# Grouped-query attention on one core: the order of the first loads, a query-major first group and zero matmuls at the start

## The chip, the core and the metric

The kernel runs on one core of a Trainium2 chip. The metric is the device time of one execution in microseconds (us), the median over several executions. Beside it stands one profiled execution, from which all durations of single instructions come. The engines are PE (matmul), ACT (activations), DVE (elementwise), POOL (elementwise) and SP (here it only issues DMAs).

## The reference

```python
B, Hq, Hkv, Sq, Sk, D = 16, 32, 8, 288, 512, 128      # q, k, v in bf16

def reference(q, k, v):
    rep = Hq // Hkv                                     # 4 query heads share one k/v head
    k = jnp.repeat(k, rep, axis=1)
    v = jnp.repeat(v, rep, axis=1)
    scores = jnp.einsum("bhqd,bhkd->bhqk", q, k) * D ** -0.5
    p = softmax(scores, axis=-1)
    return jnp.einsum("bhqk,bhkd->bhqd", p, v)
```

## The kernel before

**Groups and steps.** A group is one k/v head of one batch with its four query heads: 128 groups (`NG`), each with 4 x 288 = 1152 query rows (`R`, nine blocks of 128) against 512 keys (`NJ` = 4 blocks of 128). The transposed scores of a group have 4 x 1152 = 4608 columns (key block times query row). They are cut into three steps (`NC`) of 1536 columns (`CH`), so there are 384 steps (`NS`) in all. Four groups (`UG`) are a unit, which is what one load of keys and one of values brings (units are called `u`); the loads of unit 0 are split into single groups.

**One step.** For step `n` PE computes scores S(n) into one of two PSUM buffers (`op_s`, L499: four matmuls, or more where block borders cut them). ACT takes exp of all 1536 columns in one instruction into `pt_sb` (`op_exp`, L541). Then PE multiplies probabilities with values for three query blocks (`op_pv`, L522: 12 matmuls of 129 columns; the last column of `v_sb` is one and yields the softmax sum). DVE takes the reciprocal of the sums (`op_rc`, L558) and writes the scaled output (`op_ev`, L569). POOL copies values into `v_sb` beside the ones (`op_vc`, L551).

**Which columns a step has.** Steps go through the 4608 columns in key-major order: step 0 of a group has key block 0 with all 1152 queries and then a part of key block 1. The last group (`LASTG`) alone is query-major: each of its steps has 384 queries against all four key blocks (`pieces`, `op_exp`), which cuts its scores into six matmuls, so that its value steps can start after one exp each. Value steps of any other group wait for all three of its exps.

**The order on PE** is S(n), then the value step of `n - LAG`, with `LAG` = 4. S(n) waits for the group's keys and queries and for exp(n - 2), which frees its PSUM buffer.

**The order of the DMAs.** All DMAs are issued by SP in one order, and SP issues in order: an instruction that waits holds back those behind it. The list `first` (L601 to L603) has the loads of groups 0 to 3: `op_k(0, 0)`, `op_q(0)`, `op_k(0, 1)`, `op_q(1)`, `op_v(0, 0)` and so on. Then comes a branch into the main block. After it SP follows the list `sp`, which is sorted by a key written by hand in units of steps:

- keys `op_k(u)` (L432) and values `op_v(u)` (L444) of a unit, three buffers (`NSLOT`); from unit 3 on each waits for its buffer. Units 1 and 2 have keys near -24 + u, ahead of everything else.
- queries `op_q(g)` (L453, a transposing DMA of 128 x 1152), twelve buffers (`NQ`). Groups 4 to 11 have negative keys too.
- stores `op_store(g)` (L467), key `NC * (g + 1) + LAG + 1.5`: it waits for the group's evictions. The output has six buffers (`NO`), so the evictions of group 6 wait for store 0.

The sort key orders the issues; it is not a time at which they wait. There is a second path for extreme inputs (`general_path`), entered by a branch at the end and not taken in these runs.

Of the kernel before, what the change touches and what calls it, by code (L numbers as in the profile page):

```python
# [8 lines left out]
BF16 = mybir.dt.bfloat16  # L9
# [278 lines left out]
def bass_standalone__gqa_softmax__near_ridge_kernel(  # L288
# [6 lines left out]
    B, Hq, Sq, D = q.shape  # L295
    _, Hkv, Sk, _ = k.shape
    P = 128
# [7 lines left out]
    TPC = 3  # L305
# [9 lines left out]
    NSLOT = 3  # L315
    NQ = 12
    NPT = 3
    NO = 6
    NS = NG * NC
    LASTG = NG - 1  # L320
# [8 lines left out]
    with ExitStack() as es:  # L329
        sem = {}  # L330

        def S(name):
            if name not in sem:
                sem[name] = es.enter_context(nc.semaphore(name))
            return sem[name]
# [1 line left out]
        flag_i = es.enter_context(nc.sbuf_tensor("flag_i", [1, 1], I32))  # L337
        block = es.enter_context(nc.Block())

        for name in ["s_go", "s_one", "s_s", "s_e", "s_pv", "s_rc", "s_ev", "s_stat", "s_bad", "s_flag", "s_vc", "s_ol", "s_ea"]:  # L340
            S(name)
        for i in range(NSLOT):
            S("us_k%d" % i)
# [5 lines left out]
            S("s_q%d" % i)  # L349
        for i in range(NO):  # L350
            S("s_o%d" % i)


        gen = ExitStack()
# [4 lines left out]
        def general(eng, key, after):  # L359

            home[key] = nc.cur_bb
            eng.br(after + key)
            with nc.body("general_" + key):
                if key == "sp":
                    eng.sem_inc(sem["s_go"], 1)
                fns[key](eng)
                eng.br("done_" + key)
            nc.switch_bb(after + key)
# [27 lines left out]
        ck_sb = main.enter_context(nc.sbuf_tensor("ck_sb", [P, 3], FP32))  # L396
        bad_sb = main.enter_context(nc.sbuf_tensor("bad_sb", [P, 2, ALONE + 1], FP32))
        one_f = main.enter_context(nc.sbuf_tensor("one_f", [P, 1], FP32))
        dum = main.enter_context(nc.sbuf_tensor("dum", [P, 2], FP32))
        ps_s = main.enter_context(nc.psum_tensor("ps_s", [P, 2, CH], FP32))  # L400
        ps_o = main.enter_context(nc.psum_tensor("ps_o", [P, 2, BANK], FP32))
# [23 lines left out]
        def op_k(u, gi=None):  # L425
            eng = nc.sync
            sl = u % NSLOT
            if u >= NSLOT:
                for (s, n) in need(eng, [("s_s", NC * UG * (u - NSLOT + 1))]):
                    eng.wait_ge(s, n)  # L430
            g0, g1 = (0, UG) if gi is None else (gi, gi + 1)
            eng.dma_start_transpose(  # L432
                kt_sb[:, sl, :, g0:g1].rearrange("d j g p -> d j (g p)"),
                k_v[(u * UG + g0) * P:(u * UG + g1) * P]
            ).then_inc(sem["us_k%d" % sl if gi is None else "s_k%d" % gi], 16)
# [12 lines left out]
        def op_q(g):  # L448
            eng = nc.sync
            if g >= NQ:  # L450
                for (s, n) in need(eng, [("s_s", NC * (g - NQ + 1))]):
                    eng.wait_ge(s, n)
            eng.dma_start_transpose(qt_sb[:, g % NQ], q_v[g * P:(g + 1) * P]).then_inc(sem["s_q%d" % (g % NQ)], 16)  # L453

        def have(kind, g):

            u = g // UG
            if u == 0:
                return ("s_%s%d" % (kind, g), 16)
            return ("us_%s%d" % (kind, u % NSLOT), 16 * (u // NSLOT + (0 if u % NSLOT == 0 else 1)))  # L460
# [17 lines left out]

        def pieces(g, i):

            if g == LASTG:
                w = TPC * P
                cuts = sorted(set(range(0, CH + 1, BANK)) | set(range(0, CH + 1, w)))
                return [(a, a // w, i * w + a % w, b - a) for a, b in zip(cuts[:-1], cuts[1:])]
            lo, hi = i * CH, (i + 1) * CH
            cuts = sorted({lo, hi} | {x for x in range(0, COLS, BANK) if lo < x < hi}
                          | {x for x in range(0, COLS, R) if lo < x < hi})
            return [(a - lo, a // R, a % R, b - a) for a, b in zip(cuts[:-1], cuts[1:])]

        def op_s(n):  # L490
            eng = nc.tensor
            g, i = n // NC, n % NC
            sl, gi = (g // UG) % NSLOT, g % UG
            waits = [have("k", g), ("s_q%d" % (g % NQ), 16 * (g // NQ + 1))]
            if n >= 2:
                waits.append(("s_e", n - 1))
            qg = qt_sb[:, g % NQ].rearrange("d t p -> d (t p)")
            for x, (c, j, r0, w) in enumerate(pieces(g, i)):
                ins = emit(eng, waits if x == 0 else [], lambda: eng.matmul(  # L499
                    ps_s[:, n % 2, c:c + w], kt_sb[:, sl, j, gi, :], qg[:, r0:r0 + w], start=True, stop=True))  # L500
            ins.then_inc(sem["s_s"], 1)
# [27 lines left out]
        def op_exp(n):  # L529
            eng = nc.scalar  # L530
            g, i = n // NC, n % NC
            waits = [("s_s", n + 1)]
            if g >= NPT:
                waits.insert(0, ("s_pv", NC * (g - NPT + 1)))
            if g == LASTG:
                w = TPC * P
                dst = pt_sb[:, g % NPT].rearrange("p (j r) -> p j r", r=R)[:, :, i * w:(i + 1) * w]
                src = ps_s[:, n % 2].rearrange("p (j r) -> p j r", r=w)
            else:
                dst, src = pt_sb[:, g % NPT, i * CH:(i + 1) * CH], ps_s[:, n % 2]  # L540
            emit(eng, waits, lambda: eng.activation(dst, src, ACTF.Exp, scale=scale)).then_inc(sem["s_e"], 1)  # L541
# [56 lines left out]
                op0=ALU.is_lt, op1=ALU.add)).then_inc(sem["s_bad"], 1)  # L598


        first = [lambda: op_k(0, 0), lambda: op_q(0), lambda: op_k(0, 1), lambda: op_q(1), lambda: op_v(0, 0)]  # L601
        first += [lambda: op_k(0, 2), lambda: op_q(2), lambda: op_v(0, 1)]
        first += [lambda: op_k(0, 3), lambda: op_q(3), lambda: op_v(0, 2), lambda: op_v(0, 3)]  # L603

        sp = []
        for u in range(1, NU):
            t = NC * UG * (u - NSLOT + 1) if u >= NSLOT else -2 * NC * UG + u
            sp.append((t + 0.5, lambda u=u: op_k(u)))
            sp.append((t + (LAG if u >= NSLOT else 0.65), lambda u=u: op_v(u)))
        for g in range(UG, NG):  # L610
            t = NC * (g - NQ + 1) + 1.2 if g >= NQ else -2 * NC * UG + g // UG + 0.51 + 0.1 * (g % UG)
            sp.append((t, lambda g=g: op_q(g)))
        for g in range(LASTG):
            sp.append((NC * (g + 1) + LAG + 1.5, lambda g=g: op_store(g)))
# [4 lines left out]
        @block.sync  # L619
        def _(eng):  # L620
            for fn in first:
                fn()
            general(eng, "sp", "main_")
            for (_, fn) in sp:
                fn()
            choose(eng, "sp")

        @block.tensor
        def _(eng):
            for n in range(NS + LAG):  # L630
                if n == NS - 3:
                    hints["pe"] = eng.mark_branch_hint_location()
                if n < NS:
                    op_s(n)
                if n >= LAG:
                    op_pv(n - LAG)
            emit(eng, [("s_ev", NS - 1), ("s_bad", 2)], lambda: eng.matmul(  # L637
                ps_o[0:1, NS % 2, 0:ALONE + 1], one_f[:], bad_sb[:, 1, :], start=True, stop=True)
            ).then_inc(sem["s_bad"], 1)
            choose(eng, "pe", behind=True)  # L640

        @block.scalar
        def _(eng):
            emit(eng, [("s_one", 1)], lambda: eng.activation(dum[:, 1:2], dum[:, 0:1], ACTF.Exp))  # L644
            general(eng, "act", "main_")
            for n in range(NS):
                op_exp(n)
            op_ev_last()
            choose(eng, "act")
# [8 lines left out]

        @block.vector
        def _(eng):  # L660
            eng.memset(dum[:], 0.0).then_inc(sem["s_one"], 1)  # L661
            eng.memset(one_f[:], 1.0)
            general(eng, "dve", "main_")
            per_b = G * NC
            w0 = NS - 1 - ALONE // TPC
            last = rl_sb[:, NG * NT - ALONE:NG * NT]
            for r in range(NS):
                op_rc(r)
                op_ev(r)
                if r % per_b == per_b - 1 and r < NS - 1:  # L670
                    op_stat(r // per_b)
                if r == w0:
                    op_stat(B - 1)
                if r == w0 + 1:
                    emit(eng, [("s_stat", B)], lambda: eng.tensor_reduce(
                        ck_sb[:, 0:1], st_sb[:, 0, :], AX.X, ALU.max))
                    eng.tensor_reduce(ck_sb[:, 1:2], st_sb[:, 1, :], AX.X, ALU.min).then_inc(sem["s_stat"], 1)
                if r == w0 + 2:
                    op_over(ck_sb[:, 0:1], ck_sb[:, 1:2], ALONE, ALONE + 1, ("s_stat", B + 1), B + 2)
            op_over(last, last, 0, ALONE, ("s_rc", NS), B + 3)  # L680
            with nc.allow_low_precision(reason="a count of at most 2048"):
                emit(eng, [("s_bad", 3)], lambda: eng.tensor_reduce(  # L682
                    flag_i[:], ps_o[0:1, NS % 2, 0:ALONE + 1], AX.X, ALU.add)).then_inc(sem["s_flag"], 1)
            choose(eng, "dve")
# [30 lines left out]
```

## Time and profile before

| What | Value |
|---|---|
| median of 10 runs | 537.02 us (533.36 to 537.54) |
| the profiled execution | 537.76 us, of which its span from first to last instruction is 536.0 |
| PE busy | 521.5 us (97%), 6152 matmuls |
| ACT busy | 518.2 us (97%), 387 instructions |
| DVE busy | 288.3 us (54%) |
| POOL busy | 73.8 us (14%) |
| granted TensorE clock, mean | 0.994 |
| first score matmul | 6.86 us after the start of the span |
| HBM read and written | 16.78 MB and 37.75 MB |

In the page's second part the span is cut into 40 slices of 13.4 us, and each digit is the busy share of one slice in tenths; the row PEclk is the clock that TensorE was granted. Lines of the timeline begin with the start and the length in us; lines of waits give the total, the count and the longest. Where engines overlap, a long busy time says little by itself: what matters is which wait ended last.

### The profile page before, as it was taken

To read this page: it belongs to the slowest core of one execution; us is meant where nothing else is said; L and a number is where in the kernel's file an instruction comes from. 1 tells how busy PE (TensorE), PEld (TensorE's weight loads), DVE (VectorE), ACT (ScalarE), POOL (GpSimd) and SP (SyncE) were. 2 spreads that over 40 slices of the span, in tenths; PEclk is the share of its full clock that TensorE was granted. 3 is DMA by queue.
4 is the path that set the end of the run, shared out by engine and by line. 5 is a ranking of instruction groups with operands and counts; after the bars stand their busy time and mean duration, and the time that the engine had idled before them with its cause. 6 is when DMAs were issued, how large, how long until landed. Compare 5 with 4: busy or idle time off the path is not lost.

```text
span 536.0 us, 14538 instructions
## 1 busy us (share of the span) xinstructions
PE 521.5 (97%) x6152; PEld 406.2 (76%) x6152; DVE 288.3 (54%) x809; ACT 518.2 (97%) x387; POOL 73.8 (14%) x133
## 2 busy tenths in 40 slices
PE   4997999999999999999999999999999999999997
PEld 1775777777777777777777777777777777777776
DVE  0543555555555555555555555555555555555555
ACT  4995999999999999999999999999999999999996
POOL 1221111210111110111100111101111101111000
PEclk9997999999999999999999999999999999999999
DMA  7999999999899999999999999998989998985212
GB/s 135 209 194 255 243 237 257 289 244 221 200 204 225 224 223 202 182 222 222 231 214 174 228 209 223 225 202 223 197 212 224 232 194 227 187 217 159 89 68 91
DMA packets 253943, 110.07 MB, mean 205 GB/s; under 512 B 220848, under 2 KB 237616, under 8 KB 253872
## 3 DMA queue, kind: packets, MB, share of 16 engines
q1 hardware_dynamic: 253872, 109.08, 91.6%
q8 instruction: 50, 0.82, 0.7%
q14 instruction: 21, 0.17, 0.1%
HBM read 16.78 MB, written 37.75 MB: 102 GB/s over the span
## 4 chain that ended last, share of the span: by engine, by line
PE 96%; DMA 2%; DVE 1%; ACT 1%; SPq 0%; issue 0%; DVEq 0%
PE ps_o L522 49%; PE ps_s L499 47%; DMA qt_sb<-in_q_dram 1%; DMA out_dram<-o_sb 1%; ACT pt_sb L541 1%; DVE o_sb L569 0%; SPq L432 0%; SPq L453 0%; DVE rl_sb L558 0%; PE ps_o L637 0%; DVE bad_sb L596 0%; DVE flag_i L682 0%; DVE bad_sb L593 0%; DVEq L418 0%
## 5 line engine op out<-in xcount | busy, mean ns | idle before, releaser
L541 ACT ACTIVATE pt_sb<-ps_s 128x1536 bf16<-128x1536 f32 x384 | 516.4, 1722 | 12.0 <-PE ps_s L499 12.0
L522 PEld LDWEIGHTS ps_o<-v_sb,pt_sb 128*128 128x128 bf16 x4596 | 295.9, 98 | 59.0 <-DVE o_sb L569 4.2
L522 PE MATMUL ps_o<-v_sb,pt_sb 128*128 128x129 bf16 x4596 | 327.5, 221 | 3.8 <-DVE o_sb L569 3.8
L499 PE MATMUL ps_s<-qt_sb,kt_sb 128*128 128x512 bf16 (+3 forms) x1542 | 317.5, 329 | 7.6 <-DMA qt_sb<-in_q_dram 6.9
L569 DVE TENSOR_TENSOR o_sb<-ps_o,rl_sb 128x384 bf16<-128x384 f32 x383 | 213.6, 558 | 18.2 <-DMA out_dram<-o_sb 4.7
L558 DVE RECIPROCAL rl_sb<-ps_o 128x3 f32<-128x3 f32 x383 | 69.3, 181 | 226.3 <-PE ps_o L522 226.3
L499 PEld LDWEIGHTS ps_s<-qt_sb,kt_sb 128*128 128x128 bf16 x1542 | 117.6, 98 | 67.4 <-DMA qt_sb<-in_q_dram 6.9
L551 POOL COPY v_sb<-vd_sb 128x512 bf16<-128x512 bf16 x128 | 73.3, 616 | 417.5 <-DMA vd_sb<-in_v_dram 390.0
L588 DVE TENSOR_REDUCE st_sb<-rl_sb 128x1 f32<-128x72 f32 (+1 forms) x16 | 3.5, 217 | 0.0
L586 DVE TENSOR_REDUCE st_sb<-rl_sb 128x1 f32<-128x72 f32 (+1 forms) x16 | 3.5, 217 | 0.0
L577 ACT ACTIVATE o_sb<-ps_s,rl_sb 128x128 bf16<-128x128 f32 x1 | 0.4, 367 | 2.3 <-DVE rl_sb L558 2.3
L644 ACT ACT_TABLE_LOAD x1 | 1.3, 1283 | 0.8 <-PEq L700 0.8
L637 PE MATMUL ps_o<-bad_sb,one_f 128*1 128x25 f32 x2 | 0.2, 184 | 1.0 <-DVE bad_sb L596 1.0
L637 PEld LDWEIGHTS ps_o<-bad_sb,one_f 128*1 128x1 f32 x2 | 0.1, 80 | 1.2 <-DVE bad_sb L596 1.2
L522 PE MATMUL ps_s<-v_sb,pt_sb 128*128 128x129 bf16 x12 | 0.9, 221 | 0.0
L522 PEld LDWEIGHTS ps_s<-v_sb,pt_sb 128*128 128x128 bf16 x12 | 0.7, 98 | 0.0
L661 DVE MEMSET dum<- 128x2 f32 x1 | 0.1, 60 | 0.9 <-PEq L700 0.9
L569 DVE TENSOR_TENSOR o_sb<-ps_s,rl_sb 128x256 bf16<-128x256 f32 x1 | 0.4, 425 | 0.0
L653 POOL MEMSET v_sb<- 128x48 bf16 x1 | 0.3, 311 | 0.3 <-POOLq L700 0.3
L682 DVE TENSOR_REDUCE flag_i<-ps_o 1x1 int32<-1x25 f32 x1 | 0.2, 170 | 0.3 <-PE ps_o L637 0.3
L644 ACT ACTIVATE dum<-dum 128x1 f32<-128x1 f32 x1 | 0.2, 202 | 0.0
L596 DVE SCALAR_TENSOR_TENSOR bad_sb<-rl_sb,bad_sb 128x24 f32<-128x24 f32 x1 | 0.2, 184 | 0.0
(11 smaller groups left out, 1.4 us busy)
## 6 DMA issues: line engine op xcount, KB each, us to landing
out_dram<-o_sb SPq DMA_DIRECT2D x127, 288.0 KB, 3.4
vd_sb<-in_v_dram SPq DMA_DIRECT2D x31, 512.0 KB, 5.1
qt_sb<-in_q_dram SPq DMA_TRANSPOSE x128, 4.6
kt_sb<-in_k_dram SPq DMA_TRANSPOSE x35, 4.7
vd_sb<-in_v_dram SPq DMA_DIRECT2D x4, 128.0 KB, 3.1
out_dram<-o_sb SPq DMA_DIRECT2D x3, 96.0 KB, 1.6
```

The source lines that it names most:

```text
L499: ins = emit(eng, waits if x == 0 else [], lambda: eng.matmul(ps_s[:, n % 2, c:c + w], kt_sb[:, sl, j, gi, :], qg[:, r0:r0 + w], start=Tru ...
L522: ins = emit(eng, waits if a == 0 and j == 0 else [], lambda: eng.matmul(outs(r)[:, a, :], pt_sb[:, g % NPT, j * R + t * P:j * R + (t + 1) ...
L541: emit(eng, waits, lambda: eng.activation(dst, src, ACTF.Exp, scale=scale)).then_inc(sem["s_e"], 1)
L551: emit(eng, waits, lambda: eng.tensor_copy(v_sb[:, sl, gi * NJ:(gi + 1) * NJ, 0:D], vd_sb[:, sl, gi].rearrange("p (j d) -> p j d", d=D))). ...
L558: emit(eng, [("s_pv", r + 1)], lambda: eng.reciprocal(rl_sb[:, TPC * r:TPC * (r + 1)].unsqueeze(2), outs(r)[:, :, D:DV])).then_inc(sem["s_ ...
L569: emit(eng, waits, lambda: eng.tensor_tensor(out=o_sb[:, g % NO, t0:t0 + n, :], in0=outs(r)[:, 0:n, 0:D], in1=rl_sb[:, TPC * r:TPC * r + n ...
L577: emit(eng, [("s_o%d" % (LASTG % NO), 16 * (LASTG // NO)), ("s_rc", NS)], lambda: eng.activation(o_sb[:, LASTG % NO, NT - 1, :], outs(NS - ...
L586: emit(eng, [("s_rc", e // TPC)], lambda: eng.tensor_reduce(st_sb[:, 0, b:b + 1], rl_sb[:, a:e], AX.X, ALU.max))
L588: eng.tensor_reduce(st_sb[:, 1, b:b + 1], rl_sb[:, a:e], AX.X, ALU.min).then_inc(sem["s_stat"], 1)
L637: emit(eng, [("s_ev", NS - 1), ("s_bad", 2)], lambda: eng.matmul(ps_o[0:1, NS % 2, 0:ALONE + 1], one_f[:], bad_sb[:, 1, :], start=True, st ...
L644: emit(eng, [("s_one", 1)], lambda: eng.activation(dum[:, 1:2], dum[:, 0:1], ACTF.Exp))
L653: eng.memset(v_sb[:, :, :, D:DV], 1.0)
```

## The change

Five things are changed, all at the start of the execution:

1. **The sort keys of loads.** Each unit's keys and values and each group's queries get a key of at least about `NC * (g - 2.5) / 1.4`, so that the list brings loads 1.4 times as fast as steps use them, mixed with the stores. The new head of `sp` is: keys of unit 1 (3.01), values of unit 1 (3.16), queries of groups 4, 5, 6 (3.21, 5.36, 7.5), store 0 (8.5), queries 7 (9.64), store 1 (11.5), keys and values of unit 2 (11.59, 11.74), queries 8 and 9 (11.79, 13.93), store 2 (14.5). From group 31 on queries have the key of before; values of a unit from 3 on keep their distance of `LAG` to its keys.
2. **Group 0's queries** are loaded by three transposing DMAs of 384 columns with a semaphore each (`op_q0`, `have_q`), in place of one of 1152.
3. **Group 0 is query-major**, as the last group is: step i needs only piece i of the queries, and has six matmuls.
4. **Eight matmuls of zeros** (512 columns each) run on PE ahead of S(0), on a buffer that DVE clears first.
5. **ACT's branch** into the main block carries a branch hint, placed ahead of ACT's first activation.

```diff
+    WARM = 8
...
-            eng.br(after + key)
+            br = eng.br(after + key)
+            if key in hints:
+                br.branch_hint(hints[key])
...
+        z_sb = main.enter_context(nc.sbuf_tensor("z_sb", [P, BANK], BF16))
...
+        def op_q0(i):
+            c0, c1 = i * TPC, (i + 1) * TPC
+            nc.sync.dma_start_transpose(qt_sb[:, 0, c0:c1], q_v[0:P, c0 * D:c1 * D]).then_inc(sem["s_qp%d" % i], 16)
+
+        def have_q(g, i):
+            if g == 0:
+                return ("s_qp%d" % i, 16)
+            return ("s_q%d" % (g % NQ), 16 * (g // NQ + (0 if g % NQ == 0 else 1)))
...
-            if g == LASTG:                       # in pieces and in op_exp
+            if g in (0, LASTG):
...
-            waits = [have("k", g), ("s_q%d" % (g % NQ), 16 * (g // NQ + 1))]
+            waits = [have("k", g), have_q(g, i)]
...
-        first = [lambda: op_k(0, 0), lambda: op_q(0), lambda: op_k(0, 1), lambda: op_q(1), lambda: op_v(0, 0)]
+        first = [lambda: op_k(0, 0)] + [lambda i=i: op_q0(i) for i in range(NC)] + [lambda: op_k(0, 1), lambda: op_q(1), lambda: op_v(0, 0)]
...
-            t = NC * UG * (u - NSLOT + 1) if u >= NSLOT else -2 * NC * UG + u
-            sp.append((t + 0.5, lambda u=u: op_k(u)))
-            sp.append((t + (LAG if u >= NSLOT else 0.65), lambda u=u: op_v(u)))
+            t = max(NC * UG * (u - NSLOT + 1) + 0.5, NC * (UG * u - 2.5) / 1.4 - 0.2)
+            sp.append((t, lambda u=u: op_k(u)))
+            sp.append((t + (LAG if u >= NSLOT else 0.15), lambda u=u: op_v(u)))
...
-            t = NC * (g - NQ + 1) + 1.2 if g >= NQ else -2 * NC * UG + g // UG + 0.51 + 0.1 * (g % UG)
+            t = max(NC * (g - NQ + 1) + 1.2, NC * (g - 2.5) / 1.4)
             sp.append((t, lambda g=g: op_q(g)))
...
+            for x in range(WARM):                # PE, ahead of S(0)
+                emit(eng, [("s_z", 1)], lambda: eng.matmul(
+                    ps_o[:, 1, :], z_sb[:, 0:P], z_sb[:], start=True, stop=True))
...
+            hints["act"] = eng.mark_branch_hint_location()
             emit(eng, [("s_one", 1)], lambda: eng.activation(dum[:, 1:2], dum[:, 0:1], ACTF.Exp))
...
+            eng.memset(z_sb[:], 0.0).then_inc(sem["s_z"], 1)      # DVE, first
             eng.memset(dum[:], 0.0).then_inc(sem["s_one"], 1)
```

## The prediction

> **What bounds the kernel now.** I read the page first, for the busy shares and the 40 slices; then the waits; then the timeline around the one slice that differs, and around the start.
>
> ```profile
> PE 521.5 (97%) x6152; PEld 406.2 (76%) x6152; DVE 288.3 (54%) x809; ACT 518.2 (97%) x387; POOL 73.8 (14%) x133
> PE   4997999999999999999999999999999999999997
> ACT  4995999999999999999999999999999999999996
> PEclk9997999999999999999999999999999999999999
> ```
>
> PE and ACT are both full except in slices 1 and 4 (13.4 us each). In the body the chain alternates 0.65 us of scores and 0.69 us of probability x value: 1.34 us per step, 384 steps, 515 us. An exp is reissued 1.34 us after the one before it (12.70, then 14.03). Both engines stand at the same pitch, and nothing in the change touches it. Only the two holes can pay.
>
> ```profile
> PE ps_s L499 <- DMA qt_sb<-in_q_dram: 6.9, 1, 6.9
> DVE o_sb L569 <- DMA out_dram<-o_sb: 4.7, 1, 4.7
> PE ps_o L522 <- DVE o_sb L569: 3.8, 2, 3.6
> ```
>
> The first is the start. The second and third are one event: an eviction waits for a *store*, and PE for the eviction. The timeline shows how it comes about (start, length, engine, line):
>
> ```profile
> 14.38 2.14 SPq L432 DMA_TRANSPOSE kt_sb<-in_k_dram  x1
> 16.57 2.97 SPq L453 DMA_TRANSPOSE qt_sb<-in_q_dram  x2
> 19.58 1.85 SPq L444 DMA_DIRECT2D vd_sb<-in_v_dram  x1
> ...
> 39.21 0.58 SPq L467 DMA_DIRECT2D out_dram<-o_sb  x1
> ...
> 39.73 0.82 PE L499 MATMUL ps_s<-qt_sb,kt_sb 128*128 128x512 bf16 x4
> 43.51 0.56 DVE L569 TENSOR_TENSOR o_sb<-ps_o,rl_sb 128x384 bf16<-128x384 f32 x1 [4.74 <-DMA out_dram<-o_sb]
> 44.13 1.48 PE L522 MATMUL ps_o<-v_sb,pt_sb 128*128 128x129 bf16 x12 [3.58 <-DVE o_sb L569]
> 45.40 1.49 PE L499 MATMUL ps_s<-qt_sb,kt_sb 128*128 128x512 bf16 x4
> 47.98 1.49 PE L499 MATMUL ps_s<-qt_sb,kt_sb 128*128 128x384 bf16 x4
> 50.11 0.81 PE L499 MATMUL ps_s<-qt_sb,kt_sb 128*128 128x512 bf16 x4
> ```
>
> Store 0 could go once group 0 is evicted (about 17.9 us), but stands in SP's in-order queue behind every load with a negative key, and goes at 39.21. Group 6 needs its buffer at 38.8. PE idles 3.58 us, and the clock falls:
>
> ```profile
> 42.50:43.00 0.50, 0.00 (x0) 0.00 (x0) 0.00 (x0) 0.00 (x0) 0.00 (x0) 0.76 0.21 18
> ```
>
> (the 0.76 is the granted clock). The scores at 39.73 and 50.11 are three steps apart: 10.38 us where 3 x 1.34 = 4.03 would do. **The store stall with its clock costs 6.35 us**: 3.7 of it is the value step that came at 44.13 instead of 40.39, and 2.65 the half clock until 49.6.
>
> **The change, part by part.** I number score steps from S(0); S(4) starts at 12.86, S(12) at 23.6, S(24) at 39.73.
>
> *Order of SP.* By the new keys, after the first list come: k1 and v1 (unit 1), q4, q5, q6, store 0, q7, store 1, k2, v2, q8, q9, store 2. Issues before store 0 at before's rows: 2.14 + 1.85 + 3 x 1.5, so it goes at about 25 instead of 39, lands 4.2 us later at 29, and is needed at about 39. Stores 1 to 3 follow at about 27, 36 and 38 and are needed at 43, 47 and 51. The stall goes: **-6.35**. The loads now behind stores: q8 issues at about 32 to 33, lands 5.4 later at 38, S(24) wants it at 41; unit 3 and q12 land near 47, wanted at 57. No wait there, with 3 us to spare at the tightest.
>
> *First list.* One query transpose (1.35 us) becomes three. A transpose of 512 columns takes 1.20 and one of 1152 takes 1.35, so one of 384 is estimated at 1.17: 3.5 with gaps 3.6, that is 2.2 us more issue, and everything behind it on SP slides by 2.2. Key rows: k0 0.81 to 2.13, pieces at 2.18, 3.40, 4.62, k(0,1) 5.84, q1 7.11 (was 4.88), v 8.52, k(0,2) 9.15, q2 10.4, q3 13.7, list done 16.1 (was 13.85), and k1, after the same 0.5 us branch, at 16.6 (was 14.38).
>
> *Ramp.* A small transpose lands 3.8 after its issue: S(0) can start at 5.9 (was 6.86), S(1) at 7.2, S(2) at 8.4. But S(3) is group 1 and waits for q1, 7.11 + 3.7 = 10.8 (was 11.20). The exps of group 0 are over by then. From there, S(4) 11.5, PV(0) once v has landed and POOL has copied it (8.52 + 3.1 + 0.6 = 12.3), S(5) after exp(3) at 13.05, S(6) at 14.4 (was 12.86 + 2 x 1.34 = 15.55; q2 is there at 14.2). Gain at S(6): 1.15 us. Group 3's q lands at 17.5, wanted at 18.4.
>
> *Zero matmuls.* They run from about 1.4 us (a memset first) at the cold pace: the cold quartet of scores took 1.48 where warm ones take 0.82 shown (0.65 in the chain), so a 512-column matmul is about 0.43 and eight are 3.4 us, over at 4.8, before any data. PE is empty then, so they cost nothing; a late memset would have to cost over 1 us to be seen. Nor are they worth much: **row against rule.** In the row, the first matmul is at 6.86 and quartets still took 1.47 at 9.86; only at 12.86 are they fast. The granted clock reads 1.00 in 5 to 10 us all the same, so I take the durations. The Trainium skill ("TensorE: Matmul & The Clock Gate", Part 1: The HAM clock gate) says the gate opens after a busy window of some 3.4 us that runs freely. Eight zeros fill exactly one window only if they start with it; so the rule speaks against a sure warm start. By the rule at its best S(0) to S(2) save 0.65 each; by the row, nothing. Either way the sum is the same: S(3) waits for q1, not for the clock. If S(3) too is cold, S(6) moves to 15.1, still hidden by what follows.
>
> *Query-major group 0.* Six score matmuls for four, same 1536 columns: three steps x 2 x a few ns, under 0.05. The exp writes in four strided runs, as the last group's does, whose exps keep their pitch (five at 523.50 in 7.14 us, five at 35.31 in 7.04). PV of group 0 still waits for all three exps. ACT's branch hint and DVE's longer memset end before the table load does (2.08): 0. The cover is the wait for data; without it, some 0.5 us.
>
> *Where the new wait is.* S(12) is the first step of group 4. It needs k1 and q4. Before, q4 followed k1 directly (issue 16.57, landing 5.4 later: 22.0, wanted at 23.6). Now v1, 512 KB, is ahead of it and all is 2.2 later. k1 16.6 to 18.75, v1 then takes 0.58 (a store's or small v's row) to 1.85 (the v1 row, in a stretch of 1.3 us in which the trace shows almost no DMA bytes, 8 GB/s at 21.0 to 21.5), so q4 issues at 19.4 to 20.7 and lands 4.4 to 5.4 later: 23.8 to 26.1. I take 25.0, nearer the v1 row since that is the same transfer. The ramp wants S(12) at 14.4 + 6 x 1.34 = 22.4. So PE and ACT wait 2.6 us, all of the ramp's 1.15 is used up, and S(12) is 25.0 - 23.6 = **1.4 us later than before** (+0.2 to +2.5). Behind this wait on PE stand PV(8) and all later work. q5 and q6 land 1.4 and 2.8 later, wanted 4 and 8 later: no further wait.
>
> *Clock in that wait.* **Row against rule** again: the same page's section "Why this matters for your kernels" allows idle gaps up to about 3 us, by which 2.6 us costs nothing. The row above shows the clock down by 42.76, 2.2 us after PE's last work at 40.55, so 2.6 can be enough, and then the price is about that of before, 2.7 us. [...]less often than not; I take 0 and keep 2.7.
>
> **Sum.** -6.35 + 1.4 + 0 = -4.95. The profiled execution took 537.76 (span 536.0 and 1.76 around it): 532.8. It lies 0.74 above the median of the runs shown, 537.02, so the forecast median is 532.1.
>
> **The rivals.**
> - *q4 late, and the clock falls* (0.24): -4.95 + 2.7 = -2.25, 534.8. For: the row at 42.76. Against: a gap one microsecond shorter than the 3.58.
> - *q4 in time* (0.15): if v1's issue and the landing are both short enough that q4 is there by 22.4, the ramp's gain stands: -6.35 - 1.15 = -7.5, 529.5. For: SP's v issues later in the trace of 0.43 us. Against: q4 would have to land 3 us after an issue at 19.4; the shortest landing of any q is 3.6.
> - *Slower* (0.09): the crowded loads before S(12) decide. If k1 takes the 4.00 us of the issue at 55.09, v1 the 2.25 of v2, and q4 lands 6.4 later as the q at 47.42 did: 16.6 + 4.0 + 2.25 + 6.4 = 29.3, 5.7 late, and with the clock's 2.7 the whole is +8.4 - 6.35 = +2.0, 539.0. It turns against the change from a q4 landing at 27.3 with the clock lost, at 30.0 without.
> - *No change that shows* (0.05): pacing is an order only; no load gets a new wait, so if the crowd merely moves (q8 over 3 us late at S(24), say), it could give back what the store stall took: 537.
> - That the zeros do not open the gate is likely and changes nothing in the sum.
>
> **Chances.** The case of the sum has 0.47 (530.8 to 533.2 by q4's bounds). 0.3% or 1.6 us is about what a measurement tells from no change: faster 0.47 + 0.24 + 0.15 = 0.86, same 0.05, slower 0.09. The range runs from the in-time case, 529.3, to above the clock case, 536.0; beyond are the last two.
>
> **What would show it.** Store 0 issues near 25 us, and the wait of L569 for out_dram is gone: step 1 right. PE's first score near 5.9 and the scores of group 1 at 10.8 with a wait for in_q_dram: the ramp. A wait of PE L499 for in_q_dram of some 2.6 us near 22.4 to 25 is the step on which size and sign hang; if q4 lands before 22.4 I am too high, if the clock is at 0.50 after it, too low. An eviction still waiting for a store, or a wait at S(24), would make the forecast wrong.

## The result: 533.12 us against 537.11, and where the time went

The changed kernel takes 533.12 us (median of 8 timed runs, 532.34 to 533.60). The kernel before, run beside it, has a median of 537.11 (28 runs). The ratio is 0.9928, with a 95% interval of 0.9912 to 0.9943. The profiled executions are 534.82 after and 537.76 before; their spans are 533.1 and 536.0. The forecast was 532.1, with 530.8 to 533.2 for its main case.

The page of the changed kernel first, the same four rows as shown of before: busy times, and the busy tenths and granted clock of 40 slices of 13.3 us.

```profile
PE 522.8 (98%) x6166; PEld 406.7 (76%) x6166; DVE 288.6 (54%) x810; ACT 518.2 (97%) x387; POOL 73.8 (14%) x133
PE   6899999999999999999999999999999999999997
ACT  5889999999999999999999999999999999999996
PEclk9989999999999999999999999999999999999999
```

The hole in slice 4 of before (PE 7, ACT 5, clock 7) is gone. Slice 2 has a smaller one (PE 8, clock 8 in slice 3). The waits of the first 80 us say whose it is (total, count, longest):

```profile
PE ps_s L514 <- DMA qt_sb<-in_q_dram: 4.8, 2, 2.5
```

No eviction waits for a store any more. PE waits twice for queries: 2.47 and 2.33 us. The timeline shows both. First the start (start, length, engine, line; L514 is the scores, L537 the value step, L556 the exp):

```profile
1.26 3.60 PE L646 MATMUL ps_o<-z_sb 128*128 128x512 bf16 x8 [1.26 <-DVE z_sb L680]
4.93 2.35 PE L514 MATMUL ps_s<-qt_sb,kt_sb 128*128 128x384 bf16 x12
7.89 0.83 PE L514 MATMUL ps_s<-qt_sb,kt_sb 128*128 128x384 bf16 x6 [0.61 <-ACT pt_sb L556]
11.19 1.46 PE L514 MATMUL ps_s<-qt_sb,kt_sb 128*128 128x512 bf16 x8 [2.47 <-DMA qt_sb<-in_q_dram]
12.04 12.19 ACT L556 ACTIVATE pt_sb<-ps_s 128x1536 bf16<-128x1536 f32 x9 [1.52 <-PE ps_s L514]
```

S(0) starts at 4.93, 1.9 us earlier than before, and S(2) is done by 8.7. Then PE stands still until q1 is there: S(3) starts at 11.19, where before it started at 11.20. These are the first weight load of S(3) and the matmuls of S(12) in the kernel before:

```profile
11.20 0.13 PEld L499 LDWEIGHTS ps_s<-qt_sb,kt_sb 128*128 128x128 bf16 x2 [0.79 <-ACT pt_sb L541]
23.61 0.82 PE L499 MATMUL ps_s<-qt_sb,kt_sb 128*128 128x512 bf16 x4
```

Now SP and PE around group 4:

```profile
17.03 1.71 SPq L438 DMA_TRANSPOSE kt_sb<-in_k_dram  x1
18.78 1.01 SPq L450 DMA_DIRECT2D vd_sb<-in_v_dram  x1
19.85 5.78 SPq L459 DMA_TRANSPOSE qt_sb<-in_q_dram  x3
...
25.44 0.81 PE L514 MATMUL ps_s<-qt_sb,kt_sb 128*128 128x512 bf16 x4 [2.33 <-DMA qt_sb<-in_q_dram]
25.68 0.58 SPq L482 DMA_DIRECT2D out_dram<-o_sb  x1
...
26.87 1.49 PE L514 MATMUL ps_s<-qt_sb,kt_sb 128*128 128x512 bf16 x4
...
29.45 1.12 PE L514 MATMUL ps_s<-qt_sb,kt_sb 128*128 128x384 bf16 x4
...
31.09 0.81 PE L514 MATMUL ps_s<-qt_sb,kt_sb 128*128 128x512 bf16 x4
```

Store 0 goes at 25.68 instead of 39.21. q4 is issued at 19.85, behind v1, and lands 5.5 us later; S(12) starts at 25.44 instead of 23.61. S(13) and S(14) are slow because in this execution the clock fell 1.2 us after PE had resumed, near 26.65:

```profile
26.50:27.00 0.50, 0.50 (x9) 0.50 (x7) 0.00 (x0) 0.50 (x1) 0.00 (x0) 0.65 1.19 246
30.00:30.50 0.50, 0.50 (x5) 0.22 (x4) 0.46 (x1) 0.00 (x0) 0.00 (x0) 0.94 0.94 224
```

(the third number from the end is the granted clock; it is 0.50 in between.) S(12) to S(15) takes 5.65 us where three steps are 4.02: 1.6 us of clock. The sum of the two profiles closes: -6.35 for the store stall, +1.83 for S(12), +1.6 for the clock is -2.9, and the spans differ by 2.9.

### The profile page after: what moved, and what is told of

Its sections match the earlier page's. It is cut to its first block, busy times and chain, and to the rows that moved or that the text cites. A ratio compares the mean times of both kernels' runs of the same rounds, so it can differ in the third digit from the quotient of the medians.

```text
span 533.1 us, 14571 instructions
## 1 busy us (share of the span) xinstructions
PE 522.8 (98%) x6166; PEld 406.7 (76%) x6166; DVE 288.6 (54%) x810; ACT 518.2 (97%) x387; POOL 73.8 (14%) x133
## 4 chain that ended last, share of the span: by engine, by line
PE 94%; SPq 3%; DMA 1%; DVE 1%; issue 0%
PE ps_o L537 48%; PE ps_s L514 46%; SPq L438 1%; DMA qt_sb<-in_q_dram 1%; SPq L459 1%; SPq L463 1%; SPq L450 1%; DVE o_sb L584 0%; DVE rl_sb L573 0%; PE ps_o L655 0%; DVE bad_sb L611 0%; DVE flag_i L702 0%; DVE bad_sb L608 0%; SPq L365 0%
## 5 line engine op out<-in xcount | busy, mean ns | idle before, releaser
L556 ACT ACTIVATE pt_sb<-ps_s 128x1536 bf16<-128x1536 f32 x384 | 516.4, 1725 | 9.0 <-PE ps_s L514 9.0
L537 PEld LDWEIGHTS ps_o<-v_sb,pt_sb 128*128 128x128 bf16 x4596 | 295.3, 98 | 55.3 <-POOL v_sb L566 0.5
L537 PE MATMUL ps_o<-v_sb,pt_sb 128*128 128x129 bf16 x4596 | 326.8, 220 | 0.3 <-DVE o_sb L584 0.2
L514 PE MATMUL ps_s<-qt_sb,kt_sb 128*128 128x512 bf16 (+3 forms) x1548 | 315.5, 327 | 5.6 <-DMA qt_sb<-in_q_dram 4.8
L514 PEld LDWEIGHTS ps_s<-qt_sb,kt_sb 128*128 128x128 bf16 x1548 | 117.8, 98 | 64.7 <-ACT pt_sb L556 3.6
L646 PE MATMUL ps_o<-z_sb 128*128 128x512 bf16 x8 | 3.6, 631 | 1.3 <-DVE z_sb L680 1.3
L537 PE MATMUL ps_s<-v_sb,pt_sb 128*128 128x129 bf16 x12 | 0.9, 220 | 0.0
L537 PEld LDWEIGHTS ps_s<-v_sb,pt_sb 128*128 128x128 bf16 x12 | 0.7, 98 | 0.0
```

The source lines that it names most:

```text
L537: ins = emit(eng, waits if a == 0 and j == 0 else [], lambda: eng.matmul(outs(r)[:, a, :], pt_sb[:, g % NPT, j * R + t * P:j * R + (t + 1) ...
L646: emit(eng, [("s_z", 1)], lambda: eng.matmul(ps_o[:, 1, :], z_sb[:, 0:P], z_sb[:], start=True, stop=True))
```

## The experiments

Every kernel below was timed beside the kernel before. Three numbers describe each: the median, the ratio to the kernel before on the same chip with its interval, and the start of S(12) in its profile, which is a single execution. Four of them (zeros in the wait for q4; one transpose; old start with q4 ahead of v1; two transposes and ACT's queue) ran on another chip than the rest, and there the kernel before has a median of 537.66 instead of 536.94 and 536.95; so between the two sets the ratios compare, and not the medians. The branch hint and the query-major order were not run alone.

### Only the new sort keys

The kernel before, with this edit alone:

```diff
-            t = NC * UG * (u - NSLOT + 1) if u >= NSLOT else -2 * NC * UG + u
-            sp.append((t + 0.5, lambda u=u: op_k(u)))
-            sp.append((t + (LAG if u >= NSLOT else 0.65), lambda u=u: op_v(u)))
+            t = max(NC * UG * (u - NSLOT + 1) + 0.5, NC * (UG * u - 2.5) / 1.4 - 0.2)
+            sp.append((t, lambda u=u: op_k(u)))
+            sp.append((t + (LAG if u >= NSLOT else 0.15), lambda u=u: op_v(u)))
...
-            t = NC * (g - NQ + 1) + 1.2 if g >= NQ else -2 * NC * UG + g // UG + 0.51 + 0.1 * (g % UG)
+            t = max(NC * (g - NQ + 1) + 1.2, NC * (g - 2.5) / 1.4)
```

> The kernel before with only the new sort keys: group 0 key-major, one transpose for its queries, no zeros, no hint. Theory (the whole gain is the removed store stall, 6.35 us with its clock; the changes at the start cost more than they bring because they push q4 back by 2.4 us): the first list ends at 13.85 as before, v1 goes ahead of q4, q4 lands at 22.7 to 23.8 against 23.6 wanted, the wait for it is 0 to 0.3 us, no clock fall: about -6.2, near 531 and faster than the whole change (533.1). Rival A (the start's edits carry part of the gain): slower than the whole change, 534 or more. Rival B (q4 is late because v1 is ahead of it and not because of the start): a wait near 1.5 us or more at S(12).

Measured: **532.19 us** (531.77 to 532.45), ratio 0.9918 (0.9894 to 0.9941). The keys alone bring all that the whole change brings. This is against rival A. It fits the theory's cause, but the near 531 that the theory expected did not come, and rival B was right that the wait is there, though it is shorter than the 1.5 us that B forecast.

```profile
24.60 0.81 PE L499 MATMUL ps_s<-qt_sb,kt_sb 128*128 128x512 bf16 x4 [0.89 <-DMA qt_sb<-in_q_dram]
```

q4 was issued at 18.20 and took 6.3 us to land. The issue of v1 ahead of it took 0.6 us, and the first list had ended 0.9 us later than in the trace of before, though it is the same list (the transpose of q1 took 2.01 us to issue instead of 1.37). So PE waits for q4 even without the slower start; the start adds some 0.8 us in these two executions (25.44 against 24.60).

### Only the changes at the start

This is the changed kernel with the four lines of keys put back (two are shown):

```diff
-            t = max(NC * UG * (u - NSLOT + 1) + 0.5, NC * (UG * u - 2.5) / 1.4 - 0.2)
+            t = NC * UG * (u - NSLOT + 1) if u >= NSLOT else -2 * NC * UG + u
...
-            t = max(NC * (g - NQ + 1) + 1.2, NC * (g - 2.5) / 1.4)
+            t = NC * (g - NQ + 1) + 1.2 if g >= NQ else -2 * NC * UG + g // UG + 0.51 + 0.1 * (g % UG)
```

> The changed kernel with the sort keys of before: pieces, query-major group 0, zeros and hint stay. Theory: the ramp is ahead by about 1.1 us at S(6), but q4 follows k1 at 18.8 and lands at 23.5 to 24, so S(12) starts about where it did before; store 0 is pushed back by 2.4 us to 41.6 while group 6 wants its buffer at the same time, so the stall grows to about 6 us of idle and the clock falls: +1.5 to +2.5, 538.5 to 539.5, slower than before. Rival (the start's edits are worth their ramp): 535 to 536.5.

Measured: **539.26 us** (538.99 to 541.05), ratio 1.0049 (1.0030 to 1.0068): slower than before. The timeline of SP, DVE and PE:

```profile
42.70 0.58 SPq L482 DMA_DIRECT2D out_dram<-o_sb  x1
...
46.21 0.56 DVE L584 TENSOR_TENSOR o_sb<-ps_o,rl_sb 128x384 bf16<-128x384 f32 x1 [6.43 <-DMA out_dram<-o_sb]
46.83 1.48 PE L537 MATMUL ps_o<-v_sb,pt_sb 128*128 128x129 bf16 x12 [5.27 <-DVE o_sb L584]
```

Store 0 goes 3.5 us later than before and the store stall grows from 3.58 to 5.27 us. S(12) starts at 24.68, 1.1 us later than before: q4, issued at 18.61, took 5.9 us to land, and the earlier S(0) is worth nothing by group 4.

### q4 ahead of v1

```diff
-            sp.append((t + (LAG if u >= NSLOT else 0.15), lambda u=u: op_v(u)))
+            sp.append((t + (LAG if u >= NSLOT else 0.25), lambda u=u: op_v(u)))
```

> The changed kernel with the values of a unit keyed 0.10 later, so that q4 is issued ahead of v1 (and q8 ahead of v2). Theory (PE waits for q4 because 512 KB of v1 stand before it): q4 issues at 18.8, lands at 23.2 to 24, wanted at 22.9, so the wait shrinks from 2.4 us to 0.3 to 1.1 and the clock holds: 1.3 to 2 us below the changed kernel's runs without a clock fall, 531 to 532. Rival (the DMA rings are full whatever the order): q4 lands at 25 all the same, no change against 533.1.

Measured: **531.82 us** (531.19 to 532.18), ratio 0.9912 (0.9889 to 0.9936). q4 issued at 18.56 and landed 4.5 later; S(12) started at 23.16, 2.3 us earlier than in the changed kernel. The median is 1.3 us lower, as expected, and all runs (up to 532.18) lie below the changed kernel's fastest, though the two ratios' intervals overlap. Part of it was given back later: between 70 and 110 us the profile has a wait that neither the kernel before nor the changed kernel has there.

```profile
DVE o_sb L584 <- DMA out_dram<-o_sb: 3.9, 3, 1.6
PE ps_o L537 <- DVE o_sb L584: 0.5, 1, 0.5
```

Stores come late again, because loads 1.4 times as fast as steps stand ahead of them.

### No zeros at the start

```diff
-    WARM = 8
+    WARM = 0
```

> The changed kernel without the eight zero matmuls (WARM = 0). Theory (group 1 waits for q1 at 11.2 and group 4 for q4 at 25.4, so a warm start is lost in these waits): within 0.3 us of the changed kernel, 533.1, though S(0) to S(2) run at half the clock longer. Rival (the zeros keep the clock up and that pays): 1 to 2 us slower than the changed kernel.

Measured: **533.62 us** (532.38 to 535.57), ratio 0.9949 (0.9931 to 0.9967). The median is 0.5 above the changed kernel's, more than the 0.3 expected, but the two ratios' intervals overlap: the zeros are not shown to matter here. In the profile S(0) starts at 5.24 and S(3) at 11.10, which is where the changed kernel has it. S(12) waited 2.91 us and started at 25.93, with the clock at 0.50 from 25.67. Four of the twelve executions, this one among them, took 535.18 to 535.57 at a mean clock of 0.997, while the seven with 1.0 took 532.38 to 534.61.

### Zeros in the wait for q4

```diff
+    FILL = 12
+    NFILL = 8
...
+            if n == FILL:                        # op_s, ahead of S(12)
+                for x in range(NFILL):
+                    emit(eng, [("s_e", n - 1)], lambda: eng.matmul(
+                        ps_s[:, n % 2, 0:BANK], z_sb[:, 0:P], z_sb[:], start=True, stop=True))
```

> The changed kernel with eight more zero matmuls (512 columns) ahead of S(12), into the score buffer that S(12) overwrites, after exp(10) has freed it: PE is busy for 1.7 us of its 2.4 us wait for q4. Theory (the wait itself costs 1.4 to 1.9 us and the clock that falls in it costs another 1.6 in the executions where it falls): S(12) starts where it did, near 25.4, S(13) and S(14) at full clock, the granted clock of every run 0.999 or 1.0, and the median 0.5 to 1.5 us below the changed kernel. Rival (the clock falls elsewhere, or costs nothing because ACT would be the bound): no change.

Measured: **533.66 us** (532.70 to 534.85), ratio 0.9931 (0.9912 to 0.9949): no gain. The expectation failed, and its profile says how: the clock had fallen earlier, in a wait of 2.23 us for q1 (0.81 is the mean of the half microsecond in which it fell to 0.50), and the ramp ran late, so that no gap was left for the zeros.

```profile
10.00:10.50 0.50, 0.00 (x0) 0.00 (x0) 0.00 (x0) 0.50 (x1) 0.00 (x0) 0.81 0.98 205
25.37 1.89 PE L516 MATMUL ps_s<-z_sb 128*128 128x512 bf16 x8
27.10 0.81 PE L520 MATMUL ps_s<-qt_sb,kt_sb 128*128 128x512 bf16 x4
```

They stood in S(12)'s way for 1.7 us. So the clock can fall in either wait, and I had looked at one.

### Zeros in both waits

```diff
+            FILL = {3: 9, 12: 7}                 # nine ahead of S(3), seven ahead of S(12)
```

> The changed kernel with zero matmuls in both of its waits: nine ahead of S(3), in the wait for q1, and seven ahead of S(12), in the wait for q4; each into the score buffer that is overwritten next. The single filler showed that the clock can fall in the first wait too. Theory (a fall of the clock costs 0.5 to 1.5 us here, less than its full price, because the wait for q4 hides a late ramp): granted clock 0.999 or 1.0 in every run, S(12) near 25.4, the median at the level of the changed kernel's runs with a full clock, 532.3 to 532.8, and a narrower spread. Rival (the clock plays no part in the changed kernel's time): 533.1 or more, since the fillers only stand in the way.

Measured: **533.20 us** (532.40 to 533.83, 16 runs), ratio 0.9939 (0.9922 to 0.9956). The granted clock was 0.999 or 1.0 in all 16 runs, as intended, and the median did not move: the rival's number. **Filling the waits brings nothing.** That the clock costs the changed kernel nothing is not shown by this, for two reasons. The fillers can stand in the way themselves: in this profile S(3) follows the last of them at 11.70, 0.5 us later than in the changed kernel (here the wait for q4 covered it). And the ten executions of the changed kernel on record do go with the clock: the two with 1.0 take 532.34 and 532.68, the three with 0.994 take 533.14 to 533.60, though all five lie inside the filler's own spread. So up to about 1 us of clock in the median stays open.

A ramp that runs late behind a cold clock can end in the same wait for q4: in the trace of the single filler S(12) could have started at 25.37, where its zeros began, against 25.44 in the changed kernel. Where the clock falls in or just after the wait for q4 itself, it is paid: in the changed kernel's profiled execution, 534.82, the slowest of the ten, and in that of the kernel without zeros.

### One transpose for group 0's queries

```diff
-        first = [lambda: op_k(0, 0)] + [lambda i=i: op_q0(i) for i in range(NC)] + [lambda: op_k(0, 1), ...
+        first = [lambda: op_k(0, 0), lambda: op_q(0), lambda: op_k(0, 1), ...
```

`have_q` goes back with it. Group 0 stays query-major; the zeros, the hint and the keys stay.

> The changed kernel with one transpose of 1152 columns for group 0's queries; query-major, zeros, hint and sort keys stay. Theory (each extra transpose pushes q1 and q4 back by 1.25 us, and PE waits for both): S(0) waits to 5.8 to 6.8, but q1 lands at 8.5 instead of 11.2, group 1 starts at about 10.5 without a wait, and q4 lands near 24.3 as in the kernel with only the new keys: 1 to 1.5 us better than the changed kernel, 531.5 to 532.3, and a shorter gap, so a clock that holds. Rival (the pieces pay because S(0) starts earlier): 534 or more.

Measured: **531.09 us** (530.58 to 531.23), ratio 0.9881 (0.9862 to 0.9899), the interval wholly below the changed kernel's: **the three transposes cost about 2 us**, more than the 1 to 1.5 expected. All 384 exps now follow one another from the first:

```profile
7.99 516.17 ACT L554 ACTIVATE pt_sb<-ps_s 128x1536 bf16<-128x1536 f32 x384 [5.61 <-PE ps_s L512]
```

S(0) starts at 6.49, 1.6 us later than with pieces, and S(12) at 23.48, 2.0 us earlier.

### The same without zeros

```diff
-    WARM = 8                                     # in the kernel with one transpose
+    WARM = 0
```

> The kernel with one query transpose for group 0, without the zeros. Here group 1 waits for nothing, so a cold start is not covered by the wait for q1. Theory: S(0) to S(2) run cold, exp(0) and exp(2) come as in the kernel with only the new keys (8.3 and 11.3 instead of 8.0 and 10.7), but S(12) still waits for q4, which hides it: within 0.4 us of the kernel with zeros, 531.1 to 531.5. Rival (zeros pay where data come early): 0.6 us or more slower, 531.7 to 532.2, like the kernel with only the new keys.

Measured: **531.51 us** (531.13 to 532.74), ratio 0.9913 (0.9883 to 0.9943), S(12) at 24.89. The median is 0.4 above the one with zeros and within the theory's 531.1 to 531.5. In its profile q4 took 7.2 us to land, against 5.3 in the kernel with zeros, so at least part of the difference in S(12) is not the clock's. But the two ran on different chips, and their ratios, 0.9913 and 0.9881, differ by some 1.7 us with intervals that overlap. Whether the zeros bring anything here, and how much, stays open.

### Old start, new keys, q4 ahead of v1

```diff
-            sp.append((t + (LAG if u >= NSLOT else 0.15), lambda u=u: op_v(u)))      # in the kernel with only the keys
+            sp.append((t + (LAG if u >= NSLOT else 0.25), lambda u=u: op_v(u)))
```

> The kernel before with only the new sort keys, and q4 keyed ahead of v1. Theory (all of the gain is the store stall; without v1 ahead of it q4 lands at 22 to 23 against 23.6 wanted): no wait for q4, S(12) at 23.6 as before, 0.5 to 1 us below the kernel with only the new keys, near 531.4, unless stores come late as in the other kernel with q4 first (evictions waited for stores 6.7 us in all, of which 0.6 reached PE). Rival (q4's landing is set by the DMA engines): 532.2, no change.

Measured: **531.42 us** (531.41 to 531.71), ratio 0.9891 (0.9872 to 0.9909). S(12) at 23.27, no wait for q4, exps without a pause from 8.32. As expected to 0.1 us: all its runs lie below those of the kernel with only the keys (from 531.77), on another chip, and the two ratios' intervals overlap.

### Two transposes and ACT's queue

```diff
-            c0, c1 = i * TPC, (i + 1) * TPC      # op_q0: now for i = 0 and 1 only, 384 and 768 columns
+            c0, c1 = i * TPC, (TPC if i == 0 else NT)
...
-            sp.append((t + (LAG if u >= NSLOT else 0.15), lambda u=u: op_v(u)))
+            sp.append((t + (LAG if u >= NSLOT else 0.25), lambda u=u: op_v(u)))
...
-            t = max(NC * (g - NQ + 1) + 1.2, NC * (g - 2.5) / 1.4)                   # and so for units
+            t = max(NC * (g - NQ + 1) + 1.2, NC * (g - 2.5) / 1.25)
...
+            op_v(0, 0, eng)                      # issued by ACT, ahead of its branch, and no more by SP
+            op_v(0, 1, eng)
```

> A version that should beat both: the changed kernel with group 0's queries in two transposes (384 and 768 columns), the values of groups 0 and 1 issued by ACT while it is idle, q4 ahead of v1, and loads paced 1.25 times as fast as steps instead of 1.4 so that stores are less late. Theory (the issue time on SP ahead of q1 and q4 is what counts): q1 is issued at 6.2 instead of 7.5 and lands at 9.8, group 1 starts at about 9.9 instead of 11.2, q4 is issued near 15 and lands at 20.5, wanted at 22: S(12) near 22, 1.2 us ahead of the kernel with q4 first, 530.5 to 531. Rival (the DMAs of ACT's queue hold up the transposes): S(3) not before 11, no gain over 531.8.

Measured: **531.48 us** (530.52 to 531.72), ratio 0.9883 (0.9863 to 0.9902). All its runs lie below the changed kernel's and below those of the kernel with only the keys (from 531.77), but it misses the 530.5 to 531 forecast for it, and the intervals of its ratio and of q4 ahead of v1 in the changed kernel (0.9889 to 0.9936) overlap.

```profile
1.26 1.16 ACTq L449 DMA_DIRECT2D vd_sb<-in_v_dram  x2
6.89 2.74 PE L513 MATMUL ps_s<-qt_sb,kt_sb 128*128 128x384 bf16 x12 [2.03 <-DMA qt_sb<-in_q_dram]
```

ACT issued the two value loads at 1.26, ahead of the first query piece, and not after its table load as I had meant; the piece landed 4.7 us after its issue instead of 2.7. S(0) came at 6.89, and PE was cold again (S(0) and S(1) took 2.74 us). S(3) followed exp(1) at 11.2: the rival's "not before 11". The next kernel but one takes the two loads back to SP, and its first piece lands after 2.8 us.

### One transpose, q4 ahead of v1, slower pace

The kernel with one transpose, with the keys of the last diff (the line of the units is changed likewise):

```diff
-            sp.append((t + (LAG if u >= NSLOT else 0.15), lambda u=u: op_v(u)))
+            sp.append((t + (LAG if u >= NSLOT else 0.25), lambda u=u: op_v(u)))
...
-            t = max(NC * (g - NQ + 1) + 1.2, NC * (g - 2.5) / 1.4)
+            t = max(NC * (g - NQ + 1) + 1.2, NC * (g - 2.5) / 1.25)
```

> The kernel with one query transpose for group 0, with q4 ahead of v1 and loads paced 1.25 instead of 1.4. Theory (the q4 wait of about 0.7 us is all that is left between the ramp and the steady pitch): S(12) near 22.7 instead of 23.5, ACT without a pause from exp(0) on, 0.4 to 0.8 us faster, 530.3 to 530.7. Rival (the ramp's pace, not q4, sets S(12) now, or stores come late as they did with q4 first and pace 1.4): 531.1 or more.

Measured: **530.56 us** (530.50 to 531.27), ratio 0.9901 (0.9867 to 0.9934). S(12) started at 23.18, only 0.3 us earlier; in this execution the ramp was late itself, with S(4) at 12.43 instead of 12.18. The median is 0.5 below the kernel with one transpose, as expected, but that one ran on the other chip, and the two ratios overlap widely and do not tell them apart. Nor do the profiles: in both all 384 exps follow one another from 7.99 (in 516.2 us), and both spans are 529.5. PE's wait of 0.40 us for q4, which this edit removes, had not reached ACT. So the rival's mechanism holds in this trace, that the ramp and not q4 sets the pace, though its 531.1 did not come.

### Two transposes, all loads on SP

The kernel with ACT's queue, without its last edit:

```diff
-            op_v(0, 0, eng)                      # back to SP, behind q1 and q2 as in the changed kernel
-            op_v(0, 1, eng)
```

> Group 0's queries in two transposes (384 and 768 columns), all loads on SP, q4 ahead of v1, pace 1.25. Theory: without ACT's DMAs ahead of it the first piece lands at 4.9 again, S(0) follows the zeros at once, exp(0) at 6.4, q1 lands at 9.7 instead of 11.2, S(3) at 9.8; q4 is issued at 18 and lands at 22.4 to 22.9, and this sets S(12): 530.2 to 530.8, equal to the kernel with one transpose and q4 first within 0.4 us, since both wait for q4. Rival (an earlier exp(0) is kept to the end): 529.5 or less.

Measured: **530.14 us** (529.86 to 531.14), ratio 0.9897 (0.9863 to 0.9932). It is the lowest median of all, and all its runs lie below every run of the changed kernel (532.34 and more). By the ratio it does not stand out: one transpose, old start with q4 ahead of v1, and the last three kernels have ratios from 0.9881 to 0.9901, with intervals that overlap. Its queries and exps:

```profile
5.07 1.46 PE L514 MATMUL ps_s<-qt_sb,kt_sb 128*128 128x384 bf16 x6 [0.22 <-DMA qt_sb<-in_q_dram]
...
10.02 1.56 PE L514 MATMUL ps_s<-qt_sb,kt_sb 128*128 128x512 bf16 x8 [1.12 <-DMA qt_sb<-in_q_dram]
...
10.87 511.91 ACT L556 ACTIVATE pt_sb<-ps_s 128x1536 bf16<-128x1536 f32 x381 [0.17 <-PE ps_s L514]
```

The first piece lands early as in the changed kernel, q1 1.2 us earlier than there, q4 3.7 us after its issue at 18.17. S(12) starts at 22.01.

### One table for all of them

From S(12) on, every kernel runs the same steps. (One difference in the order of loads lasts to the end: with the new keys the values of a unit stand 4 behind its keys, where they stood 3.5, so one query transpose goes ahead of them. Behind 120 us the waits of PE are the same before and after, 1.2 us in all.) So the span less the start of S(12) should be one number, unless something stalls later. All from the profiled executions, in us:

| Kernel | S(12) starts | span | span less S(12) |
|---|---|---|---|
| two transposes on SP | 22.01 | 528.1 | 506.1 |
| changed, q4 first | 23.16 | 529.9 | 506.7 (stores late) |
| one transpose, q4 first | 23.18 | 529.5 | 506.3 |
| old start, keys, q4 first | 23.27 | 529.7 | 506.4 |
| one transpose | 23.48 | 529.5 | 506.0 |
| two transposes, ACT's queue | 23.64 | 530.0 | 506.4 |
| only the keys | 24.60 | 530.7 | 506.1 |
| one transpose, no zeros | 24.89 | 530.9 | 506.0 |
| changed, both waits filled | 25.73 | 531.8 | 506.1 |
| changed, filler at S(12) | 27.10 | 533.1 | 506.0 |
| changed, no zeros | 25.93 | 533.5 | 507.6 (clock falls there) |
| changed | 25.44 | 533.1 | 507.7 (clock falls there) |
| before | 23.61 | 536.0 | 512.4 (store stall) |
| only the start | 24.68 | 538.6 | 513.9 (longer store stall) |

Ten kernels agree within 0.7 us. What distinguishes all fourteen is when S(12) starts, whether the clock falls in the wait ahead of it, and whether the evictions of group 6 wait for store 0. Nothing else that the change does is seen to reach the end in these executions, one of each kernel.

## Why the prediction was right, step by step

- *The store stall goes.* Right. Store 0 issued at 25.68 (about 25 forecast), and no eviction waits for a store. Its worth of 6.35 us in the profiled execution agrees with the table: 512.4 less 506.1 is 6.3, so nothing of it is caught up later.
- *Three transposes cost 2.2 us of issue.* Right in kind, a little small: they took 1.25, 1.25 and 1.40 rather than 1.17, 3.99 in all, so 2.6 more than one.
- *A piece lands 3.8 us after its issue.* In the profiled execution 2.7, and S(0) started at 4.93 instead of 5.9. In the other profiles with the same three pieces the first landed after 2.8 to 3.8 us, so 3.8 is the upper end and not wrong. It made no difference, since group 1 waits for q1 as forecast (11.19 against 10.8).
- *The zeros cost nothing and are worth little.* No run contradicts it. They ended at 4.86, so with pieces landing at 4.9 the assumed spare time after them was almost nil, and S(0) still ran cold (the first exp came 1.45 us after S(0) began). S(1) was fast: the two together took 2.35 us. With the same zeros S(0) took 0.83 us in the profile of only the start's edits, and S(0) and S(1) took 2.74 us with q4 ahead of v1. So zeros give a warm start in some executions only, as was said of the rule; the wait for q1 made it irrelevant.
- *The new wait for q4.* Right: 2.33 us where 2.6 was forecast, S(12) 1.83 us later than before where 1.4 was. q4 was there at 25.4, where I took 25.0: its issue at 19.85 was inside the forecast, its 5.5 us to landing just outside. The ramp was late too, with S(3) at 11.19 instead of 10.8 and S(12) wanted at 23.1 instead of 22.4. That the wait came out so near is in part luck, since both its ends moved. For *q4 in time* the prediction took 3.6 us as the shortest landing of any query; over the whole trace of before it is 3.2, which puts q4 at 22.6 and leaves that case out of reach all the same.
- *The clock in that wait.* I took 0 and kept 2.7. In the profiled execution 1.6 was paid, after PE had resumed; how much the median pays, between nothing and about 1 us, is open. What was missed is a second wait, for q1, in which the clock can fall as well, and that a fall there can be hidden. Of the two rules weighed, the Trainium skill's allowance of gaps up to about 3 us ("TensorE: Matmul & The Clock Gate", Why this matters for your kernels) did not hold in the profiled execution: the gap was 2.33 us by the record and the clock fell all the same, as it did in the gap of 2.23 us ahead of S(3) in the trace of the single filler. The row of before (2.2 us) was the better guide to what can happen.
- *The sum.* -4.95 forecast, -4.0 measured in the medians. Of the difference, 0.4 is q4's landing. The rest lies in the kernel before: my sum took the store stall from a profile with a granted clock of 0.994. In 53 runs of before shared with the experiments, 17 had 0.994 (median 537.85), 27 had 0.997 (536.87) and 9 had 1.0 (534.50). The median of before therefore pays about 1 us less for the clock than the execution that I measured it on. With 5.4 instead of 6.35, and 1.8 for S(12), the sum is -3.6; this is an estimate, and it brackets the -4.0 from the other side; the last 0.4 us is not explained.
- *The rivals.* The slower case came to be in one experiment, though by another mechanism: the start's edits alone, which lengthen the store stall.

## What to carry to other kernels

On a queue that issues in order, ask of every load what stands ahead of it and when its consumer wants it; splitting one load to start earlier pushes all those behind it back by a whole issue time, here 1.25 us each, and the first consumer of the pushed load can give the gain back, as S(3) did here. Also ask whether a wait reaches the engine that sets the pace: where the exps already ran without a pause, removing PE's wait for q4 left the span as it was. To see what an edit at the start is worth, find the first step after which all versions run alike, and compare when that step begins. A stall whose price includes a fallen clock should be priced over several executions, since the clock of one profile need not be that of the median.

## What the runs showed that I had not expected

- **A transpose of the same size lands between 3.1 and 9.3 us after its issue**, over the fourteen profiles. q4 took 3.7, 4.5, 5.3, 5.5, 6.3 and 7.2 us in six of the kernels. In the changed kernel's trace, with q4 issued at 19.85, the DMA engines moved 55 to 70 GB/s for about 1 us around its issue, and 287 after it (the last two columns are the DMA share and GB/s):

```profile
19.00:19.50 0.50, 0.50 (x6) 0.26 (x5) 0.35 (x2) 0.50 (x1) 0.27 (x1) 1.00 1.14 70
19.50:20.00 0.50, 0.50 (x11) 0.43 (x9) 0.39 (x1) 0.50 (x1) 0.00 (x0) 1.00 0.38 55
20.00:20.50 0.50, 0.50 (x10) 0.38 (x8) 0.04 (x1) 0.50 (x2) 0.46 (x1) 1.00 1.26 287
```

  The same trace has one 16 KB packet of the instruction queue by 18.6 us, and the trace of before has such a packet between 19 and 20 with its own lull at 20.5 to 21.5 (60 and 8 GB/s). That the lull comes from instruction fetch is argued from two places in time only; no run tested it.
- **The kernel before has three levels of time and not one**, and they go with the granted clock: 534.50, 536.87 and 537.85 us at 1.0, 0.997 and 0.994. In the one that was traced, at 0.994, the fall lies in the store stall and lasts 6.8 us (42.76 to 49.6). The changed kernel's trace has one of half that length (26.65 to 30.06). At half clock 6.8 us take 0.006 from the mean of 536 us, and 3.4 us take 0.003: the levels fit a fall of 6.8 us, one of 3.4 us and none. This is an estimate; no execution of before at the other two levels was traced.
